# Linear attention and a rational feed-forward layer: the first four attention chunks worked whole, and the decoded words' scratch in PSUM

## The chip, the cores and the metric

The kernel runs on one core of one Trainium2 chip. The metric is the device time of one execution in microseconds, the median of several runs. The core has TensorE (PE; its weight loads are listed as PEld), VectorE (DVE), ScalarE (ACT), GpSimd (POOL) and SyncE (SP, which here issues all data transfers). Each works through its own list of instructions in order and waits on semaphores for the others.

## What is computed

Attention with a decaying state over 4 batches, 8 heads, 768 tokens and 64 dimensions per head, and then a feed-forward layer over the 3072 tokens (512 to 2048 to 512) with a rational function in place of an activation:

```python
for t in range(S):                      # gamma: one decay per head
    state = gamma * state + outer(k[t], v[t])
    y[t] = scale * q[t] @ state
...
h = x @ w_in
P = a[0] + a[1]*h + a[2]*h*h + a[3]*h*h*h
Q = 1.0 + abs(b[0])*abs(h) + abs(b[1])*h*h
out = (P / (Q + 1e-06)) @ w_out
```

## The kernel before

**Attention** goes in 24 chunks of 128 tokens (6 for each batch; `NSTEP`). For chunk i the words of the written order are: `q`/`Q` scale the queries (`scale_q`, on POOL or on DVE), `v` scales the values (POOL), `s` decays the state (POOL), `S` the scores on PE, `M` the causal mask on DVE (PSUM to SBUF), `R` and `r` the recall (state times query) on PE, `V` the masked scores times the values on PE, `O` the outer product of keys and values on PE, `C` the carry of the state on DVE, `X` and `Y` the high and low parts of the result, rounded on ACT and subtracted on DVE. A chunk is cut into two halves of 64 tokens, so that four 64 x 64 matmuls fill the quarters of the PE array, with a state at the beginning (`begin`) and one in the middle (`middle`) of the chunk. The results of 4 chunks are one block of 512 tokens (`x_block`); there are 6 blocks.

**The feed-forward layer** goes in 96 slots: one block of 512 tokens with one of the 16 slices of 128 hidden columns. In slot k, `I` is the first product (`gemm_in`, 12 matmuls into a bank `ph0` or `ph1`), `a`, `b`, `c`, `e` are steps of the rational function on ACT, `p` on POOL, `f` (`poly_vector`) and `H` (`ratio_vector`) on DVE, `g` and `K` split the result into a high and a low part (ACT, POOL), and `Z` is the second product (`gemm_out`, 12 matmuls into the banks `po0` to `po3`), three slots later. `H` ends with the line p (L422), the last reader of the slot's `ph` bank.

**The weights** come as 32 tiles of 64-bit floats. For tile j: `t` reads a byte of each word on ACT (L135), `u` reads the upper word on ACT (L143), `d` joins them on DVE in two operations (L153, u from u and t; L156, t from the raw words and u), `h` rounds on ACT (L166), and `l` takes the rest on POOL (L173). Slot k's `I` needs tiles, `Z` others, in the order of the list `tiles`.

**The order** is written out by hand: `BEGIN` lists the words up to slot 12 with 19 tiles decoded, and each engine gets its instructions in that order. `fill` words are matmuls on zeros whose result nobody reads. After `BEGIN`, `run()` takes the other slots by a rule; there each part of attention stands between two products. On SP a prelude issues the loads of chunks 0 to 5 with `FIRST[i]` weight tiles after chunk i's, up to 11 tiles; later loads are the words `load` and `fetch`, and a load waits on SP until its buffer's last reader is done, with all that stands behind it.

**PSUM** has 8 banks: `po0` to `po3`, `ph0`, `ph1`, and a pair (`pair`). Before, chunks 0 to 3 use `po0`/`po1` and `po2`/`po3` in turn as their pair, the outer products of chunks 0 to 4 use `ph0` and `ph1`, and the scratch `u` of the 19 tiles of `BEGIN` lies in SBUF in buffers of the tag `o`. In `run()` the scratch of the other 13 tiles lies in the pair of the latest chunk (`spare`).

## Time and profile before

| | |
|---|---|
| median of 3 runs | 642.82 us (640.2 to 643.7) |
| the profiled execution | 640.74 us, of it 638.5 us span |
| mean granted TensorE clock | 0.992 |
| PE busy | 606.3 us (95%), 5300 matmul rows |
| DVE busy | 458.9 us (72%), 711 |
| ACT busy | 444.4 us (70%), 723 |
| POOL busy | 363.3 us (57%), 304 |
| data moved | 53.05 MB, mean 83 GB/s |

The span runs from the first to the last instruction. Shares of busy time are means over the whole span; the kernel's beginning and the rest of it look different, so they are read by stage. "A <- B: 5.1" in a list of waits is the idle time of an engine just before A that ended when B was done. A float32 matmul of the attention shows as two rows.

### The profile page before, as it was taken

Reading aid. Unit: us, or ns where it says so; the run is one execution under the profiler, and the core shown is the slowest. Engines: PE = TensorE matmul, PEld = TensorE weight load, DVE = VectorE, ACT = ScalarE, POOL = GpSimd, SP = SyncE. Lnnn points to the kernel's source line nnn. Section 1 sums busy time; section 2 is a strip of 40 time slices with the busy share of each in tenths; the row PEclk is TensorE's granted clock in tenths of the full one; section 3 lists DMA queues with packets and bytes.
Section 4 is the critical chain, followed back from the end, with each engine's and each line's share of the span. In section 5 each row is a group of like instructions: output and inputs, shape, how many; then the busy total and the mean of one; then the engine's idle time right before and its main releaser. Section 6 shows DMA issues by size and latency. Waiting matters only on the chain.

```text
span 638.5 us, 13103 instructions
## 1 busy us (share of the span) xinstructions
PE 606.3 (95%) x5300; PEld 487.2 (76%) x5306; DVE 458.9 (72%) x711; ACT 444.4 (70%) x723; POOL 363.3 (57%) x304
## 2 busy tenths in 40 slices
PE   7588788899999999999999999999999999999997
PEld 3476566688887787788888888888888888888885
DVE  3589999788997776767666666666676666666664
ACT  2278897899987655666667667676666666777773
POOL 3369777688887654546546356545555534444442
PEclk9899899999999999999999999999999999999999
DMA  8958390300302324302202212202121000100001
GB/s 285 377 179 325 135 362 2 132 1 0 132 0 69 124 68 133 128 6 67 67 1 59 80 54 67 69 2 67 47 87 59 3 1 0 39 28 1 2 1 66
DMA packets 24716, 53.05 MB, mean 83 GB/s; under 512 B 3280, under 2 KB 3280, under 8 KB 24656
## 3 DMA queue, kind: packets, MB, share of 16 engines
q1 hardware_dynamic: 24656, 52.22, 23.5%
q8 instruction: 41, 0.67, 0.4%
q14 instruction: 19, 0.16, 0.1%
HBM read 43.82 MB, written 8.39 MB: 82 GB/s over the span
## 4 chain that ended last, share of the span: by engine, by line
PE 75%; DVE 6%; ACT 4%; issue 2%; POOLq 0%; DVEq 0%; ACTq 0%
PE ph L387 36%; PE po L443 35%; PE pair L345 1%; PE pair L297 1%; PE pair L312 1%; PE pair L268 1%; DVE p L411 1%; DVE u L153 1%; DVE q L420 1%; DVE p L422 1%; DVE o L462 1%; ACT s L405 1%; DVE ph L421 1%; ACT p L407 1%; DVE p L412 1%
## 5 line engine op out<-in xcount | busy, mean ns | idle before, releaser
L387 PE MATMUL ph<-xh,w 128*128 128x512 f32 (+2 forms) x776 | 210.6, 393 | 13.8 <-DVE p L422 12.8
L406 POOL TENSOR_TENSOR q<-q,s 128x512 f32<-128x512 f32 x84 | 109.3, 1302 | 198.0 <-ACT s L405 194.3
L443 PE MATMUL po<-w,gh 128*128 128x512 f32 x768 | 199.8, 392 | 0.0
L387 PEld LDWEIGHTS ph<-xh,w 128*128 128x128 f32 x776 | 143.3, 189 | 46.5 <-DVE p L422 14.8
L443 PEld LDWEIGHTS po<-w,gh 128*128 128x128 f32 x768 | 142.8, 188 | 30.2
L411 DVE TENSOR_TENSOR p<-ph,p 128x512 f32<-128x512 f32 x96 | 66.2, 689 | 85.0 <-ACT p L407 84.1
L399 ACT ACTIVATE q<-ph 128x512 f32<-128x512 f32 x84 | 50.2, 597 | 101.4 <-PE ph L387 101.4
L428 POOL TENSOR_TENSOR gl<-p,gh 128x512 fp32r<-128x512 f32 x85 | 110.4, 1299 | 4.7 <-issue 3.3
L443 PE MATMUL po<-w,gl 128*128 128x512 f32 x384 | 110.8, 390 | 1.0 <-POOL gl L533 0.7
L387 PE MATMUL ph<-xl,w 128*128 128x512 f32 (+2 forms) x388 | 104.0, 390 | 0.0
L420 DVE SCALAR_TENSOR_TENSOR q<-q,qcon,ph 128x512 f32<-128x512 f32 x96 | 71.5, 745 | 40.3 <-ACT ph L417 39.1
L443 PEld LDWEIGHTS po<-w,gl 128*128 128x128 f32 x384 | 72.0, 188 | 17.3 <-POOL gl L533 1.7
L387 PEld LDWEIGHTS ph<-xl,w 128*128 128x128 f32 x388 | 73.1, 189 | 15.6
L416 ACT ACTIVATE s<-q,qcon 128x512 f32<-128x512 f32 x96 | 69.5, 724 | 20.8 <-POOL q L406 19.4
L412 DVE SCALAR_TENSOR_TENSOR p<-p,par_sb,ph 128x512 f32<-128x512 f32 x96 | 71.8, 748 | 3.4
L421 DVE SCALAR_TENSOR_TENSOR ph<-p,par_sb,ph 128x512 f32<-128x512 f32 x96 | 71.9, 749 | 0.0
L422 DVE SCALAR_TENSOR_TENSOR p<-q,ph 128x512 f32<-128x512 f32 x96 | 65.9, 686 | 3.3
L417 ACT ACTIVATE ph<-s 128x512 f32<-128x512 f32 x96 | 57.8, 602 | 9.9 <-DVE p L412 0.8
L407 ACT ACTIVATE p<-ph,par_sb 128x512 f32<-128x512 f32 x84 | 64.2, 764 | 0.0
L405 ACT ACTIVATE s<-q,babs 128x512 f32<-128x512 f32 x72 | 58.8, 817 | 2.4
L173 POOL TENSOR_TENSOR w<-t,w 128x512 fp32r<-128x512 f32 x32 | 42.8, 1340 | 25.4 <-ACT w L166 17.5
L427 ACT CAST gh<-p 128x512 fp32r<-128x512 f32 x85 | 52.0, 612 | 7.5 <-DVE p L422 7.2
(55 smaller groups left out, 540.2 us busy)
## 6 DMA issues: line engine op xcount, KB each, us to landing
raw<-in_w_in SPq DMA_DIRECT2D x16, 512.0 KB, 8.0
raw<-in_w_out SPq DMA_DIRECT2D x16, 512.0 KB, 8.4
kT<-in_kT SPq DMA_DIRECT2D x24, 256.0 KB, 4.1
qT<-in_qT SPq DMA_DIRECT2D x24, 256.0 KB, 4.2
v<-in_v SPq DMA_DIRECT2D x24, 256.0 KB, 3.1
out<-o SPq DMA_DIRECT2D x24, 256.0 KB, 2.1
k<-in_k SPq DMA_DIRECT2D x20, 256.0 KB, 3.7
half<-o SPq DMA_DIRECT2D x8, 256.0 KB, 2.4
```

The costliest lines, as they stand in the source:

```text
L387: nc.tensor.matmul(ph[:, t0:t1], w1[f][:, part, kt * P : (kt + 1) * P], x[:, kt, t0:t1], start=(i == 0), stop=(i == 3 * NP - 1),)
L405: nc.scalar.activation(s, q, AF.Identity, bias=babs[:, 0:1], scale=babs[:, 1:2])
L406: nc.gpsimd.tensor_mul(q, q, s)
L407: nc.scalar.activation(p, ph, AF.Identity, bias=par_sb[:, 2:3], scale=par_sb[:, 3:4])
L411: nc.vector.tensor_mul(p, ph, p)
L412: nc.vector.scalar_tensor_tensor(p, p, par_sb[:, 1:2], ph, ALU.add, ALU.mult)
L416: nc.scalar.activation(s, q, AF.Abs_reciprocal_sqrt, bias=qcon[:, 0:1])
L420: nc.vector.scalar_tensor_tensor(q, q, qcon[:, 0:1], ph, ALU.add, ALU.mult)
L421: nc.vector.scalar_tensor_tensor(ph, p, par_sb[:, 0:1], ph, ALU.add, ALU.mult)
L422: nc.vector.scalar_tensor_tensor(p, q, 2.0, ph, ALU.subtract, ALU.mult, reverse0=True)
L428: nc.gpsimd.tensor_sub(gl, p, gh.bitcast(F32))
L443: nc.tensor.matmul(o_tiles[n][tt], g_[:, tt * P : (tt + 1) * P], w2[f][:, part], start=(first and m == 0), stop=(last and m == 2),)
```

## The change

- `by_chunk`: chunks 0 to 3 are worked whole, with new functions. A chunk has 8 matmuls each for scores (64 x 128 by 128 columns), recall, values (128 x 64 by 128) and outer product, one recall in place of two, no middle state, and a mask of 128 x 128 for each head (`causal_sb` is 192 columns wide in place of 64). The masked scores lie in buffers of the tags `p` and `s`.
- PSUM: scores of chunks 0 to 3 lie in `po0` and `po1`, their outer products in `ph0`, their results in the one `pair`; the outer product of chunk 4 lies in `po0` and `po1`; `fill` writes `po3`.
- The scratch `u` of each tile has a bank named in the order (`u6@po0`), or a bank of the latest pair (`pair0`, `pair1`, `half0`).
- `zeros` lies in a buffer of the tag `o`.
- `FIRST`: tile 1 is fetched after chunk 1's loads.
- The queries of chunks 1 to 3 are scaled on POOL (`q1` to `q3`), not on DVE (`Q1` to `Q3`).
- `BEGIN` is a new order of the same slots, chunks and tiles, with 30 fill matmuls in place of 46.

```diff
--- before.py
+++ after.py
@@ -69,18 +69,23 @@
 
     def pair(i):
         if i not in pairs:
-            if 0 <= i < SPB:
-                pairs[i] = [early_bank("pair", f"po{r + 2 * (i % 2)}") for r in range(2)]
-            else:
-                both = early_bank("pair", "pair").rearrange("p (b x) -> p b x", b=2)
-                pairs[i] = [both[:, r] for r in range(2)]
+            both = early_bank("pair", "pair").rearrange("p (b x) -> p b x", b=2)
+            pairs[i] = [both[:, r] for r in range(2)]
+            if i >= SPB:
                 spare.append(both.bitcast(U32))
         return pairs[i]
 
     def u_place(i, place):
 
-        if place is None:
-            return in_halves(ff.tile([P, TB], U32, name="u", tag="o", bufs=BUFS["o"]))
+        if isinstance(place, str) and place[:4] == "pair":
+            if not spare:
+                both = early_bank("scratch", "pair", U32)
+                spare.append(both.rearrange("p (b x) -> p b x", b=2))
+            return in_halves(spare[-1][:, int(place[4:])])
+        if isinstance(place, str) and place not in ("whole", "half0"):
+            return in_halves(early_bank("u", place, U32))
+        if place == "half0":
+            return spare[-1][:, :, : TB // 2]
         if place == "whole":
             return spare[-1][:, i % 2].rearrange("p (b x) -> p b x", b=2)
         return spare[-1][:, :, place * (TB // 2) : (place + 1) * (TB // 2)]
@@ -89,7 +94,7 @@
         return x.rearrange("p (b x) -> p b x", b=2)
 
 
-    causal_sb = const.tile([P, HP], F32, name="causal_sb")
+    causal_sb = const.tile([P, HP + P], F32, name="causal_sb")
     qdec_sb = const.tile([P, NP, P], F32, name="qdec_sb")
     vdec_sb = const.tile([P, H], F32, name="vdec_sb")
     sdec_sb = const.tile([P, NP], F32, name="sdec_sb")
@@ -97,7 +102,7 @@
     babs = const.tile([P, 2], F32, name="babs")
     qcon = const.tile([P, 1], F32, name="qcon")
     lcon = const.tile([P, 1], F32, name="lcon")
-    zeros = const.tile([P, TB], BF16, name="zeros")
+    zeros = ff.tile([P, TB], BF16, name="zeros", tag="o", bufs=BUFS["o"])
     wp = ctx.enter_context(tc.tile_pool(name="wp", bufs=1))
     w1, w2 = {}, {}
 
@@ -257,7 +262,7 @@
     def outer(i):
         if i >= NSTEP:
             return
-        banks = [early_bank("pk", f"ph{b}") for b in range(2)] if i <= SPB else pair(i - 1)
+        banks = [early_bank("pk", f"po{b}") for b in range(2)] if i == SPB else pair(i - 1)
         pk = [x[:, : TB // 2].rearrange("p (h d) -> p h d", d=D) for x in banks]
         st = steps[i]
         st["pk"] = pk
@@ -284,6 +289,88 @@
             steps.setdefault(i + 1, {})["from", 0] = state
             nc.vector.tensor_add(state, st["pk"][1], st["from", 1])
 
+    def whole_outer(i):
+        st = steps[i]
+        st["pk"] = early_bank("pk", "ph0")[:, : TB // 2].rearrange("p (h d) -> p h d", d=D)
+        for aj in range(NP):
+            for r in range(2):
+                h = head(aj // 2, r, aj % 2)
+                nc.tensor.matmul(
+                    st["pk"][half(r), aj], st["k"][:, h], st["v"][:, h],
+                    start=True, stop=True, skip_group_check=True,
+                )
+    def whole_carry(i):
+        state = at.tile([P, NP, D], F32, name="begin")
+        steps.setdefault(i + 1, {})["from", 0] = state
+        if i % C == 0:
+            nc.vector.tensor_copy(state, steps[i]["pk"])
+        else:
+            nc.vector.tensor_add(state, steps[i]["pk"], steps[i]["from", 0])
+    def whole_scores(i):
+        st = steps[i]
+        pa = st["pa"] = [
+            early_bank("pa", f"po{r}").rearrange("p (n t) -> p n t", t=P) for r in range(2)
+        ]
+        for n in range(NP):
+            for r in range(2):
+                nc.tensor.matmul(
+                    pa[r][:, n], st["kT"][half(r), n], st["qT"][half(r), n],
+                    start=True, stop=True, skip_group_check=True,
+                )
+    def whole_mask(i):
+        st = steps[i]
+        for r in range(2):
+            st["aT", r] = ff.tile([P, NP, P], F32, name="aT", tag="ps"[r])
+            nc.vector.tensor_mul(
+                st["aT", r], st["pa"][r],
+                causal_sb[:, HP:].unsqueeze(1).broadcast_to([P, NP, P]),
+            )
+    def whole_px(i, r):
+        return pair(i)[r][:, : TB // 2].rearrange("p (a t) -> p a t", t=P)
+    def whole_recall(i):
+        st = steps[i]
+        for a in range(2):
+            for j in range(2):
+                for r in range(2):
+                    nc.tensor.matmul(
+                        whole_px(i, r)[half(j), a],
+                        st["from", 0][half(r), 2 * a + j], st["qT"][half(r), 2 * a + j],
+                        start=opens(i, r, j), stop=False, skip_group_check=True,
+                    )
+    def whole_values(i):
+        st = steps[i]
+        for a in range(2):
+            for j in range(2):
+                for r in range(2):
+                    nc.tensor.matmul(
+                        whole_px(i, r)[half(j), a],
+                        st["v"][:, head(a, r, j)], st["aT", r][:, 2 * a + j],
+                        start=opens(i, r, j), stop=True, skip_group_check=True,
+                    )
+    def whole_x(i, r):
+        t = slice((i % SPB) * P, (i % SPB + 1) * P)
+        xh, xl = (
+            y.rearrange("p (a r) t -> p a r t", r=2)[:, :, r, t] for y in x_block(i // SPB)
+        )
+        return whole_px(i, r), xh, xl
+    def whole_x_high(i):
+        for r in range(2):
+            x, xh, _ = whole_x(i, r)
+            nc.scalar.copy(xh, x)
+    def whole_x_low(i):
+        for r in range(2):
+            x, xh, xl = whole_x(i, r)
+            nc.vector.tensor_sub(xl, x, xh.bitcast(F32))
     def px(i, kh):
         return pair(i)[kh][:, TB // 2 :].rearrange("p (a r t) -> p a r t", a=2, r=2)
 
@@ -321,7 +408,7 @@
             st["aT", r] = at.tile([P, NP, HP], F32, name="aT")
             x = nc.vector.tensor_mul(
                 st["aT", r], st["pa"][r],
-                causal_sb.unsqueeze(1).broadcast_to([P, NP, HP]),
+                causal_sb[:, :HP].unsqueeze(1).broadcast_to([P, NP, HP]),
             )
             if ordered and r == 1:
                 after(x, st["recalled"])
@@ -493,9 +580,12 @@
 
 
         def fill(n):
-            bank = early_bank("fill", "pair" if SPB not in pairs else "po0")
+            bank = early_bank("fill", "po3")
             for _ in range(n):
-                nc.tensor.matmul(bank[:, :TB], zeros[:, :P], zeros, start=True, stop=True)
+                nc.tensor.matmul(bank, zeros[:, :P], zeros, start=True, stop=True)
+        def by_chunk(whole, halves):
+            return lambda i: (whole if i < SPB else halves)(i)
 
         def gemm_in_begin(k):
             if k == 0:
@@ -548,17 +638,17 @@
             "Q": lambda i: scale_q(i, nc.vector),
             "v": scale_v,
             "s": scale_state,
-            "O": outer,
-            "C": carry,
-            "S": scores,
-            "R": lambda i: recall(i, True),
-            "M": lambda i: mask(i, True),
-            "V": values,
+            "O": by_chunk(whole_outer, outer),
+            "C": by_chunk(whole_carry, carry),
+            "S": by_chunk(whole_scores, scores),
+            "R": by_chunk(whole_recall, lambda i: recall(i, True)),
+            "M": by_chunk(whole_mask, lambda i: mask(i, True)),
+            "V": by_chunk(whole_values, values),
             "r": lambda i: recall(i, False),
-            "X": x_high_both,
-            "Y": x_low_both,
+            "X": by_chunk(whole_x_high, x_high_both),
+            "Y": by_chunk(whole_x_low, x_low_both),
             "t": decode_low,
-            "u": lambda j: decode_high(j, None),
+            "u": decode_high,
             "d": decode_join,
             "h": decode_split,
             "l": decode_rest,
@@ -579,8 +669,9 @@
             "y": lambda k: store_first(k - 1, 1),
         }
         for word in BEGIN.split():
+            word, *place = word.split("@")
             name = word.rstrip("0123456789")
-            emit[name](int(word[len(name) :]))
+            emit[name](int(word[len(name) :]), *place)
 
     def run():
 
@@ -688,25 +779,25 @@
 }
 BUFS = {"gh": 3, "gl": 3, "o": 4}
 FETCH = 11
-FIRST = (1, 0, 1, 1, 2, 2)
+FIRST = (1, 1, 1, 1, 2, 2)
 LAG = 3
 BEGUN = {"slots": 12, "tiles": 19}
 
 BEGIN = """
-t0 u0 d0 h0 Q0 l0 fill18 S0 v0 fill3 O0 n0 v1 C0 s1 fill2 R0 O1 M0 Q1 fill1 V0 v2 r0 S1 C1 X0 Y0
-s2 fill1 R1 O2 M1 Q2 fill2 V1 t1 r1 S2 C2 X1 u1 s3 fill1 R2 Y1 v3 M2 d1 fill3 O3 V2 r2 Q3 h1 C3
-X2 fill1 S3 l1 t2 Y2 R3 s4 u2 M3 v4 d2 fill3 V3 q4 r3 O4 X3 C4 h2 fill1 S4 t3 Y3 l2 I0 u3 t4 s5
-d3 v5 u4 R4 d4 J0 h3 l3 I1 a0 M4 h4 c0 q5 t5 f0 b0 l4 V4 a1 r4 u5 O5 p0 load6 fetch3 c1 C5 X4 d5
-e0 Y4 h5 H0 b1 fill7 S5 l5 R5 t6 p1 t7 M5 u6 fill3 I2 q6 t8 f1 u7 g0 v6 d6 e1 K0 V5 d7 a2 r5 h6
-Z0 load7 fetch1 fetch1 c2 l6 H1 h7 b2 l7 t9 f2 fetch1 O6 g1 p2 I3 X5 C6 u8 K1 e2 Y5 fetch1 d8 v7
-u9 Z1 a3 s7 t10 d9 q7 h8 c3 fetch1 H2 l8 b3 S6 h9 R6 p3 t11 M6 I4 g2 fetch1 l9 f3 u10 u11 K2 t12
-d10 e3 Z2 fetch1 d11 h10 u12 l10 H3 h11 a4 l11 V6 t13 fetch1 r6 b4 O7 load8 d12 I5 c4 p4 X6 C7
-h12 fetch1 f4 s8 g3 l12 u13 t14 Y6 K3 Z3 e4 d13 fetch1 a5 v8 H4 t15 c5 S7 R7 h13 fetch1 b5 M7
-l13 I6 u14 f5 g4 p5 t16 d14 u15 fetch1 K4 e5 Z4 d15 a6 u16 H5 c6 fetch1 b6 V7 r7 h15 p6 O8 f6
-h14 I7 X7 l15 fetch1 g5 d16 e6 l14 Y7 h16 K5 Z5 H6 a7 fetch1 t17 b7 l16 c7 C8 I8 g6 p7 f7 u17
-fetch1 t18 K6 d17 e7 s9 Z6 a8 H7 fetch1 h17 c8 l17 b8 f8 g7 I9 p8 u18 fetch1 d18 K7 e8 h18 Z7 H8
-a9 l18 c9 b9 f9 g8 p9 I10 w8 y8 K8 e9 H9 a10 c10 b10 f10 I11 g9 p10 K9 e10 Z8 a11 H10 c11 b11
-f11 p11 g10 K10 e11 H11 load9 q8 v9
+t0 u0@ph1 d0 h0 Q0 l0 fill20 S0 v0 M0 fill2 O0 v1 V0 C0 s1 O1 X0 C1 q1 Y0 s2 t1 fill4 S1 v2
+u1@po2 R1 M1 n0 O2 d1 V1 q2 X1 C2 fill1 S2 s3 h1 Y1 l1 t2 M2 R2 u2@ph1 v3 d2 fill1 V2 O3 q3 X2
+C3 h2 Y2 s4 t3 fill2 S3 l2 u3@po2 R3 M3 I0 v4 d3 q4 V3 h3 t4 l3 O4 X3 C4 u4@po3 Y3 v5 t5 d4 S4
+u5@po2 s5 J0 d5 q5 h4 R4 I1 a0 c0 M4 l4 h5 f0 t6 l5 b0 V4 u6@po0 r4 p0 O5 t7 load6 fetch3 d6 X4
+u7@po1 C5 Y4 h6 e0 l6 d7 S5 R5 a1 M5 t8 q6 H0 h7 V5 c1 r5 load7 fetch1 fetch1 t9 l7 b1 f1 I2 v6
+u8@po3 g0 d8 p1 u9@po2 fetch1 t10 K0 d9 e1 O6 q7 h8 C6 Z0 h9 fetch1 H1 a2 l8 X5 c2 l9 b2 Y5 I3
+fetch1 g1 f2 s7 u10@pair1 K1 t11 d10 u11@pair0 v7 Z1 t12 fetch1 d11 a3 p2 h10 c3 l10 b3 f3 S6
+fetch1 e2 p3 R6 M6 t13 H2 V6 e3 r6 fetch1 O7 load8 h11 X6 H3 l11 I4 g2 K2 t14 fetch1 C7 g3 Y6 K3
+Z2 a4 u12@pair1 s8 c4 fetch1 d12 v8 b4 u13@pair0 f4 I5 p4 h12 u14@pair1 l12 fetch1 d13 e4 d14
+t15 Z3 h13 a5 H4 l13 fetch1 h14 c5 l14 t16 S7 f5 R7 g4 I6 t17 fetch1 K4 M7 b5 u15@half0 p5 d15
+Z4 a6 fetch1 e5 c6 H5 b6 V7 fetch1 h15 p6 r7 O8 f6 g5 I7 l15 X7 C8 e6 fetch1 K5 Y7 t18 H6 Z5 s9
+a7 u16@pair1 b7 fetch1 d16 c7 p7 g6 I8 u17@pair0 f7 K6 h16 fetch1 u18@pair1 d17 l16 e7 Z6 d18 a8
+h17 c8 l17 H7 b8 h18 p8 f8 g7 I9 l18 e8 K7 H8 Z7 a9 c9 b9 f9 g8 p9 I10 w8 y8 K8 e9 H9 a10 c10
+b10 f10 I11 g9 p10 K9 e10 Z8 a11 H10 c11 b11 f11 p11 g10 K10 e11 H11 load9 q8 v9
 """
 
 
@@ -736,7 +827,9 @@
     par = _np.concatenate([inputs["moe_a"], inputs["moe_b"]])
     gamma = 1.0 - 2.0 ** (-5.0 - _np.arange(H, dtype=_np.float64))
     t = _np.arange(P, dtype=_np.float64)
-    causal = (t[:, None] % (P // 2)) <= t[None, : P // 2]
+    causal = _np.concatenate(
+        [(t[:, None] % (P // 2)) <= t[None, : P // 2], t[:, None] <= t[None, :]], axis=1
+    )
     heads = gamma.reshape(2, 2, 2)
     by_row = _np.repeat(heads.transpose(1, 0, 2).reshape(2, NP), D, axis=0)
     arrays = {
```

## The prediction, made before the changed kernel was run

> **What bounds the kernel now.** I read the busy tenths of the page first, then the busy time by stage, then the chain of waits. One digit below is a fortieth of the span (16 us).
>
> ```profile
> PE   7588788899999999999999999999999999999997
> DVE  3589999788997776767666666666676666666664
> ```
>
> VectorE (DVE) is full in slices 3 to 7, while TensorE (PE) has gaps; from slice 9 PE is full. Cut at the marks that matter (41.04: end of mask M4; 118.24: end of H9, the last rational step ahead of slot 11's product):
>
> ```profile
> core 0: us, PE busy (x) PEld busy (x) DVE busy (x) ACT busy (x) POOL busy (x), PEclk, DMA share, GB/s
> 0.00:12.20 12.20, 8.45 (x98) 3.82 (x99) 3.01 (x8) 3.63 (x6) 3.47 (x7) 1.00 0.86 262
> 12.20:41.04 28.84, 21.37 (x550) 16.75 (x549) 19.16 (x38) 10.43 (x22) 14.70 (x14) 0.88 0.86 317
> 41.04:118.24 77.20, 62.70 (x650) 47.55 (x650) 73.34 (x102) 66.62 (x114) 56.41 (x44) 0.98 0.54 199
> 118.24:183.00 64.76, 64.71 (x285) 53.59 (x286) 55.74 (x82) 57.72 (x95) 52.30 (x46) 1.00 0.14 49
> ```
>
> In the third stage DVE is 95% busy, ScalarE (ACT) 86%, PE 81%. From 118.24 on PE is 100% busy. The chain of waits shows how the one turns into the other (start, us, what):
>
> ```profile
> 94.91 1.66 DVE u L153
> ...
> 117.55 0.70 DVE p L422
> ...
> 118.29 3.02 PE ph L387 x12
> 121.31 2.72 PE po L443 x12
> ```
>
> The chain runs on DVE until p L422, the end of H9, which frees the PSUM bank that slot 11's product waits for; after it, the chain is PE, product after product. So the end is the end of H9 plus PE work that this change leaves alone. What H9 gains or loses, the kernel gains or loses.
>
> **The change part by part.**
>
> *The scratch u of all 19 early tiles moves from SBUF into PSUM banks.* The old kernel holds both forms already, the PSUM one in its later slots (min/median/max in ns):
>
> ```profile
> L153 DVE SCALAR_TENSOR_TENSOR u<-u,t x19: 681/894/1800, 6.1 to 108.3; 128x512 uint32<-128x512 uint32 x19
> L153 DVE SCALAR_TENSOR_TENSOR pair<-pair,t x13: 692/700/700, 130.2 to 197.7; 128x512 uint32<-128x512 uint32 x13
> L156 DVE SCALAR_TENSOR_TENSOR t<-raw,u x19: 691/989/1669, 6.8 to 109.0; 128x512 uint32<-128x512 uint32 x19
> L156 DVE SCALAR_TENSOR_TENSOR t<-raw,pair x13: 686/687/689, 130.9 to 198.4; 128x512 uint32<-128x512 uint32 x13
> L143 ACT ACTIVATE u<-raw x19: 650/670/691, 5.4 to 107.6; 128x512 f32<-128x512 f32 x19
> L143 ACT ACTIVATE pair<-raw x13: 602/614/643, 126.7 to 197.1; 128x512 f32<-128x512 f32 x13
> ```
>
> With u in SBUF the two joins stretch up to 1.8 us; in PSUM they never do. They stretch while GpSimd (POOL) works, whose operation (1.28 undisturbed) stretches too:
>
> ```profile
> 34.31 1.28 POOL L173 TENSOR_TENSOR w<-t,w 128x512 fp32r<-128x512 f32 x1 [3.93 <-ACT w L166]
> 38.09 1.73 POOL L173 TENSOR_TENSOR w<-t,w 128x512 fp32r<-128x512 f32 x1
> 38.72 1.66 DVE L156 SCALAR_TENSOR_TENSOR t<-raw,u 128x512 uint32<-128x512 uint32 x1
> ```
>
> POOL is 81% busy (52.30 of 64.76) in the stage that holds most of the PSUM joins, so they are steady beside a busy neighbour. Sums over the first 185 us (x19) and over the third stage (x14), busy us and mean ns:
>
> ```profile
> L156 DVE SCALAR_TENSOR_TENSOR t<-raw,u 128x512 uint32<-128x512 uint32 x19 | 21.1, 1110 | 0.9
> L153 DVE SCALAR_TENSOR_TENSOR u<-u,t 128x512 uint32<-128x512 uint32 x19 | 20.2, 1063 | 5.0 <-ACT u L143 5.0
> L156 DVE SCALAR_TENSOR_TENSOR t<-raw,u 128x512 uint32<-128x512 uint32 x14 | 16.4, 1170 | 0.7
> L153 DVE SCALAR_TENSOR_TENSOR u<-u,t 128x512 uint32<-128x512 uint32 x14 | 15.5, 1108 | 0.1
> ```
>
> A PSUM pair of joins costs 0.700 + 0.687 = 1.387 us. All 19: 41.3 - 26.4 = 14.9 us off DVE; 31.9 - 14 x 1.387 = 12.5 of it in the third stage, 2.5 before. ACT saves 0.056 us a tile.
>
> *Chunks 0 to 3 whole.* Each mask is 2 operations of 512 columns in place of 256, the carry one operation in place of two, and the q scaling of chunks 1 to 3 goes from DVE to POOL.
>
> ```profile
> L322 DVE TENSOR_TENSOR aT<-pair,causal_sb 128x256 f32<-128x256 f32 x16 | 6.0, 416 | 3.0 <-PE pair L297 3.0
> L227 DVE TENSOR_TENSOR qT<-qT,qdec_sb 128x512 f32<-128x512 f32 x4 | 2.7, 684 | 0.0
> L281 DVE TENSOR_TENSOR middle<-pk,begin 128x256 f32<-128x256 f32 x4 | 1.7, 424 | 6.3 <-PE pair L297 5.1 <-PE pk L268 1.3
> L227 POOL TENSOR_TENSOR qT<-qT,qdec_sb 128x512 f32<-128x512 f32 x5 | 7.4, 1473 | 0.0
> ```
>
> The 512-column mask is not in the trace: it lies between 0.416 (no longer than now) and 2 x 0.416 = 0.83; I take 0.684, the other 512-column multiply. DVE: masks 8 x 0.268 = +2.1, carries 4 x -0.424 = -1.7, scaling 3 x -0.684 = -2.1. POOL gets at most 3 x 1.47 = 4.4 more in a stage where it had 14.70 of 28.84, so there it becomes as tight as DVE. On PE scores, values, outer and the two recalls go from 16 matmuls each (recalls 8 + 8) to 8, but scores and values now also compute the 64-token cross blocks, twice the product. PE isn't the bound there, so I take zero and keep both ends below. All four chunks now share one pair of banks (they alternated over po0 to po3): recall i+1 waits for the low half (Y) of chunk i, with values and outer behind it on PE; the longer mask on DVE covers that (0.7 us if not).
>
> *What the opening waited for.* The idle time of DVE between 12.20 and 41.04 is 28.84 - 19.16 = 9.7 us (us in total, times, longest):
>
> ```profile
> DVE middle L281 <- PE pair L297: 5.1, 2, 4.4
> DVE aT L322 <- PE pair L297: 3.0, 1, 3.0
> DVE middle L281 <- PE pk L268: 1.3, 1, 1.3
> PE pair L297 <- issue: 3.2, 1, 3.2
> q8 instruction: 41, 0.67, 0.4%
> PE 606.3 (95%) x5300; PEld 487.2 (76%) x5306; DVE 458.9 (72%) x711; ACT 444.4 (70%) x723; POOL 363.3 (57%) x304
> ```
>
> These are waits for PE, and PE itself once stood 3.2 us in the middle of one recall, waiting for nothing shown. The instruction queue q8 moved 41 packets for 10,606 PE and weight-load rows, 259 each: I read the stall as a packet of PE instructions that was late behind the data transfers (DMA share 0.86). A whole chunk has half the rows (some 128 in place of 256), so two of four packets go. [...]
>
> So M4's end: 41.0, less DVE work (2.5 stretch, 2.1 scaling, 1.7 carries, minus 2.1 masks, minus 1.4 for the joins of tile 5, which now stand ahead of M4) = 2.8, less about half of the 9.4 us of waits, as the rows halve: 33.5. Bounds: 38 (waits stay) and 29. The floor is the loads: ahead of chunk 4's last byte lie 4 raw tiles (one more than before, tile 1's fetch is moved ahead of chunk 2 on SP's queue and delays chunks 2 to 4 by 0.5 MB), 5 chunks of 1.05 MB, the decay table and the mask, now 0.1 MB: 7.7 MB; 3.2 MB land by 12.2 at 262 GB/s and the rest at 317 to 400 by 24 to 26, then q4, scores and mask add 3. Chunk 5's loads wait for chunk 1's values, which don't come later.
>
> *The third stage.* DVE: 73.34 - 12.5 - 1.4 (tile 5) = 59.4. ACT: one tile's three operations and one linear term stand ahead of M4 now (2.4 start to start), and 13 x 0.056 = 0.7: 66.62 - 3.1 = 63.5. POOL: below 56.41. PE: 62.70, less two fills. ACT is the longest now: what goes off DVE is not all won, since ACT is next at 63.5. Two engines that feed each other, both near full, will not do as well as one: I take ACT at 95%, what DVE reached: 66.8. Bounds: 64.5 and 63.5 / 0.86 = 73.6 (ACT no better used than now).
>
> *The rest.* BEGIN issues the same loads, fetches, slots and tiles, in another order; load6, load7 and load8 still stand behind V4, V5, V6 and the fetches behind them, and move with these. Fills fall by 16 matmuls; they only filled gaps (if the clock sinks for that: a 3.9 us gap is in the old trace too). The zeros tile and the fill bank po3 cost nothing: po3 is next used by tile 4's u, after the last fill. outer of chunk 4 uses po0 and po1, whose masks are done. After H9 the order is unchanged: zero, 0 to 2 us if ACT is behind there.
>
> *Sum.* H9 ends at 33.5 + 66.8 = 100.3 in place of 118.24: 17.9 us less. The profiled execution took 640.74 (span 638.5 and 2.2 around it), 2.1 below the median of 642.82. 640.7 - 17.9 = 622.8.
>
> **The rivals.**
>
> *ACT becomes the bound as loosely as it is used now.* For: it must serve DVE, PE and POOL in one fixed order; it waited on DVE 86% used. Against: much of its idle time was waiting for stretched joins. Stage 73.6: H9 at 107.1, 629.6.
>
> *The opening stays as late as its waits.* Either PE stalls for its instructions as before, or it pays for the new shapes. After an attention block a product takes 2.95 in place of 2.72 us:
>
> ```profile
> 301.80 2.95 PE ph L387 x12
> 304.75 2.72 PE po L443 x12
> ```
>
> A whole chunk changes shape about four times (64 x 128, 64 x 64, 128 x 64, fills): 16 x 0.23 = 3.7 us. M4 then ends at 37.5 to 38, H9 at 105: 627.3. [...]
>
> *The scratch banks serialize ACT and DVE, and it is slower.* From tile 10 on u alternates over pair0 and pair1, and its write on ACT must wait until the joins of the tile before it in that bank are done; behind it in ACT's queue stand a, b, c, e of the slots. If each of 13 tiles cost ACT a full turn, 1.39 + 0.61 = 2.0 us, the stage is 63.5 + 26 = 89.5, H9 at 123: 645.5. It turns to a loss once a tile costs over 1.7 us. Against: where the old kernel has u in the pair, DVE waited little for it:
>
> ```profile
> DVE pair L153 <- ACT pair L143: 6.1, 12, 1.2
> ```
>
> 0.5 us each, and tiles 6 to 9 have four banks.
>
> *No change:* only if the joins stretch in PSUM too in this stage; then 12.5 us come back and the opening's gain is half lost: 639.
>
> **How the numbers follow.** Forecast 623: 0.62, own range 616 to 628. ACT loose, 630: 0.17. Late opening, 627: 0.11. Serialized, 645: 0.06. No change: 0.04. Half a per cent (3.2 us) is about what a measurement of this kernel can tell from none. Faster 0.90, same 0.04, slower 0.06. The range takes in the first three with their bounds: low 616 (M4 at 30, stage 64.5: 23.7 less is 617, and one for the run), high 634 (M4 at 38 with a stage of 73.6: 634.1).
>
> **What would show it.** Joins at 0.69 to 0.70 us with little spread right from the start; POOL's operations at 1.3. M4 ending at 30 to 36; no long PE stall inside chunks 2 and 3. Between M4 and H9 ACT at least as busy as DVE, 65 to 70 us long. I11 starting near 100, and PE solid from there. The prediction is wrong if the joins stretch against POOL with PSUM operands; if ACT stands before its u writes waiting for DVE's joins; or if PE shows idle time after I11 that it did not have.

## The result and the profile after

The changed kernel takes 632.44 us (631.41 to 634.66, 4 runs) beside 641.51 us for the kernel before in the same comparison: ratio 0.986, 95% interval 0.982 to 0.991. It is 1.4% faster, clear of the noise and inside the outer range of 616 to 634, but outside the 616 to 628 that went with the forecast of 623: 9 us were won where 18 were forecast. The profiled execution took 634.66 us (span 632.9), 2.2 above the median.

Page of the changed kernel, busy tenths of PE, DVE and the granted clock:

```profile
PE   8779898999999999999999999999999999999997
DVE  3668788789887766766667667666666666766663
PEclk9978899999999999999999999999999999999999
```

Busy time by stage, cut at the same marks (M4 now ends at 37.78, H9 at 112.15; columns as before: PE, PEld, DVE, ACT, POOL, granted clock, DMA share, GB/s):

```profile
0.00:12.20 12.20, 10.50 (x86) 5.50 (x86) 4.08 (x9) 3.68 (x7) 4.15 (x8) 1.00 0.79 263
12.20:37.78 25.58, 19.66 (x293) 15.83 (x291) 15.97 (x32) 12.26 (x26) 17.75 (x17) 0.91 0.97 357
37.78:112.15 74.37, 64.26 (x647) 50.96 (x646) 60.26 (x101) 63.91 (x110) 49.27 (x41) 0.92 0.57 207
112.15:183.00 70.85, 70.79 (x312) 58.55 (x313) 61.02 (x91) 63.37 (x105) 57.84 (x51) 1.00 0.14 45
```

From H9 to the end lie 632.9 - 112.15 = 520.8 us, before 638.5 - 118.24 = 520.3: the end is H9 plus a constant, as the prediction had it. DVE has 60.26 us of work in the third stage (59.4 forecast), ACT 63.91 (63.5). The work was forecast right. The stage is 74.4 long in place of 66.8, M4 4.3 late, H9 11.9 late.

The joins and POOL's operation (min/median/max in ns):

```profile
L158 DVE SCALAR_TENSOR_TENSOR pair<-pair,t x22: 692/700/700, 59.9 to 191.6; 128x512 uint32<-128x512 uint32 x22
L158 DVE SCALAR_TENSOR_TENSOR u<-u,t x10: 690/692/700, 5.7 to 51.7; 128x512 uint32<-128x512 uint32 x10
L161 DVE SCALAR_TENSOR_TENSOR t<-raw,u x10: 686/688/701, 6.4 to 52.5; 128x512 uint32<-128x512 uint32 x10
L178 POOL TENSOR_TENSOR w<-t,w x32: 1272/1292/1328, 7.9 to 197.1; 128x512 fp32r<-128x512 f32 x32
```

The stretch is gone, on both engines, from the first tile on. What got worse is the clock: 0.92 in the third stage in place of 0.98. Four PE operations of the timeline (idle time and its releaser in brackets), the granted clock behind them (PE busy, clock, DMA share, GB/s), and two products of the chain of waits:

```profile
32.81 0.76 PE L399 MATMUL pair<-qT,kT 64*64 64x64 f32 x32 [1.98 <-POOL begin L250]
45.26 0.69 PE L399 MATMUL pair<-qT,kT 64*64 64x64 f32 x32 [2.53 <-DMA k<-in_k]
47.10 1.13 PE L432 MATMUL pair<-aT,v 64*64 64x64 f32 x32 [0.92 <-DVE aT L409]
66.55 0.69 PE L432 MATMUL pair<-aT,v 64*64 64x64 f32 x32 [1.99 <-DVE aT L409]
```

```profile
34.00:38.00 4.00, 4.00 (x30) 0.50 0.62 247
50.00:54.00 4.00, 4.00 (x11) 0.53 1.01 364
66.00:70.00 4.00, 3.13 (x75) 0.68 0.43 131
```

```profile
49.15 5.16 PE ph L474 x12
...
112.21 3.02 PE ph L474 x12
```

PE stands 2.0 to 2.5 us before S4, S5 and V6, where the new order has no fills (the old one had one ahead of S4, seven ahead of S5 and none ahead of V6). Behind S4 the clock is granted at half until 40 us (0.50 from 34 to 40), and behind V6 for the next 3 to 4 us (0.50 from 68 to 70, 1.00 from 71 on); behind S5 it stays near full (0.96 from 45.3 to 47.1) until a second gap, 0.92 us before V5, and is half from there to 54 us (0.50 from 47.1 to 50, then 0.53). Product I2 takes 5.16 us in place of 3.02. The releaser named for S5 is doubtful: in this trace and in those of experiments 4 and 6 S5 starts 0.26 us after Y4 ends on DVE, the last reader of the pair that S5 writes.

### The profile page after: what moved, and what is told of

It is laid out like the page before. It is cut to its first block, busy times and chain, and to the rows that moved or that the text cites. A ratio compares the mean times of both kernels' runs of the same rounds, so it can differ in the third digit from the quotient of the medians.

```text
span 632.9 us, 12567 instructions
## 1 busy us (share of the span) xinstructions
PE 608.2 (96%) x5032; PEld 491.4 (78%) x5034; DVE 443.5 (70%) x704; ACT 443.9 (70%) x723; POOL 360.2 (57%) x307
## 4 chain that ended last, share of the span: by engine, by line
PE 78%; DVE 8%; ACT 4%; issue 2%; POOLq 0%; POOL 0%; DVEq 0%; ACTq 0%
PE ph L474 38%; PE po L530 35%; PE pair L432 1%; PE pair L384 1%; PE pair L273 1%; PE pair L399 1%; DVE q L507 1%; DVE ph L508 1%; DVE pair L158 1%; DVE p L509 1%; DVE p L498 1%; DVE t L161 1%; DVE o L549 1%; ACT s L492 1%; ACT pair L148 1%
## 5 line engine op out<-in xcount | busy, mean ns | idle before, releaser
L474 PE MATMUL ph<-xh,w 128*128 128x512 f32 (+2 forms) x776 | 213.6, 398 | 6.4 <-DVE p L509 5.3
L474 PEld LDWEIGHTS ph<-xh,w 128*128 128x128 f32 x776 | 145.9, 192 | 39.3 <-DVE p L509 7.8
L530 PEld LDWEIGHTS po<-w,gh 128*128 128x128 f32 x768 | 142.8, 188 | 30.2
L474 PE MATMUL ph<-xl,w 128*128 128x512 f32 (+2 forms) x388 | 105.4, 394 | 0.0
L507 DVE SCALAR_TENSOR_TENSOR q<-q,qcon,ph 128x512 f32<-128x512 f32 x96 | 71.5, 745 | 41.8 <-ACT ph L504 40.6
L474 PEld LDWEIGHTS ph<-xl,w 128*128 128x128 f32 x388 | 74.4, 193 | 15.9
L503 ACT ACTIVATE s<-q,qcon 128x512 f32<-128x512 f32 x96 | 69.3, 722 | 21.7 <-POOL q L493 19.2
L499 DVE SCALAR_TENSOR_TENSOR p<-p,par_sb,ph 128x512 f32<-128x512 f32 x96 | 71.8, 748 | 3.4
L178 POOL TENSOR_TENSOR w<-t,w 128x512 fp32r<-128x512 f32 x32 | 41.3, 1295 | 20.0 <-ACT w L171 12.1
```

The lines of the kernel that those rows point to most:

```text
L474: nc.tensor.matmul(ph[:, t0:t1], w1[f][:, part, kt * P : (kt + 1) * P], x[:, kt, t0:t1], start=(i == 0), stop=(i == 3 * NP - 1),)
L499: nc.vector.scalar_tensor_tensor(p, p, par_sb[:, 1:2], ph, ALU.add, ALU.mult)
L503: nc.scalar.activation(s, q, AF.Abs_reciprocal_sqrt, bias=qcon[:, 0:1])
L507: nc.vector.scalar_tensor_tensor(q, q, qcon[:, 0:1], ph, ALU.add, ALU.mult)
L530: nc.tensor.matmul(o_tiles[n][tt], g_[:, tt * P : (tt + 1) * P], w2[f][:, part], start=(first and m == 0), stop=(last and m == 2),)
```

## The experiments

Times are medians, ratios go against the kernel before of the same comparison. "Stage" is M4 to H9 in the profiled execution. DVE lines have other numbers in some kernels.

**1. The scratch alone, in the old order and halves.**

```diff
-u3 ... u4 ... u8 ... u9 ... u18
+u3@po1 ... u4@po2 ... u8@half0 ... u9@pair0 ... u18@pair1   (13 of 19 tiles)
```

> The old order, halves and loads as before; the scratch u of 13 of the 19 early tiles lies in PSUM (tiles 3 to 10, 13, 14, 15, 17, 18), which are the ones whose joins stretched most: in the old trace their 26 joins took 11.4 us more than 0.69 to 0.70 us each. Theory A (the stretch of the joins against POOL was what VectorE lost, and it was the bound): VectorE's busy time between M4 and H9 falls by about 11 us and H9 comes 7 to 11 us earlier, limited by ScalarE at 66 us in that stage; time about 632 to 635, that is nearly all that the whole change brought. Theory B (the new order and the whole chunks bring the gain, the joins only overlap better): within 2 us of the old kernel, 640 to 643.

636.17 us, ratio 0.993 [0.991, 0.995]. DVE has 63.97 us in the stage (73.34 before), H9 ends at 113.6, 4.6 earlier, where theory A asked for 7 to 11. Nine microseconds less work on DVE gave half of that.

**2. The new order, scratch back in SBUF.**

```diff
+ if place is None: return in_halves(ff.tile([P, TB], U32, name="u", tag="o", ...))
- u3@po2 ... u18@pair1
+ u3 ... u18
```

> The new kernel with its order, its whole chunks and its loads, but with the scratch u of all 19 early tiles back in SBUF (four buffers). Theory A: the joins stretch again to 0.9 to 1.1 us in the mean, 10 to 15 us more VectorE work ahead of H9, and the gain goes: 638 to 646. Theory B: joins stretch, but ScalarE and TensorE bound the stage, so the time stays at 632 to 635.

639.52 us, ratio 0.998 [0.996, 1.000]: without the scratch in PSUM nearly nothing is left. DVE is back at 70.51 in the stage, but the clock is 0.87 there, so the price of the scratch is mixed with the clock's (experiment 12 parts them). Here and in experiment 12 `zeros` is a tile of its own again, 128 columns wide, which a fill reads four times over.

**3. The new order and scratch, chunks 0 to 3 in halves.**

```diff
- "S": by_chunk(whole_scores, scores), "M": by_chunk(whole_mask, ...), ...
+ "S": scores, "M": lambda i: mask(i, True), "V": halves_values, ...
```

> The new order, loads and PSUM scratch, but chunks 0 to 3 worked in halves of 64 tokens as before (outer products in po0 and po1, scores in the pair; C0 and R0 stand ahead of M0). Theory A1 (whole chunks save packets of TensorE instructions, 3 us): M4 ends some 3 us later, 635 to 636. Theory A2 (whole chunks cost TensorE more array time than they save): each chunk's products take about 0.7 us less on TensorE, time within 2 us of the new kernel's 632, or below it.

640.59 us (636.4 to 643.7), ratio 0.998 [0.995, 1.001], slower than both theories have it. M4 ends at 40.0, at a clock of 0.85 up to there. Again the clock is mixed in.

**4. The changed kernel with 26 more fills at the new gaps.**

```diff
-d4 S4 ... d7 S5 ... h7 V5 ... f1 I2
+d4 fill8@ph0 S4 ... d7 fill10@po3 S5 ... h7 fill4@po3 V5 ... f1 fill4@po3 I2
```

> The new kernel with 26 more matmuls on zeros, where TensorE stood idle in the new trace: 8 ahead of S4 (bank ph0), 10 ahead of S5, 4 ahead of V5, 4 ahead of I2 (bank po3). Theory C (the new order lost 5 to 6 us to the halved TensorE clock: I1 took 4.4, I2 5.2, in place of 2.9): granted clock between 30 and 62 us near 1.0, I1 and I2 at 2.9 to 3.1, time 626 to 629. Theory D (these products only fill time in which VectorE and ScalarE are late anyway): clock up, but H9 within 1.5 us of the new kernel's 112, time 631 to 634.

629.89 us (629.07 to 630.47), ratio 0.983 [0.981, 0.985]. The granted clock of its profiled execution, at the places where it had been half:

```profile
34.00:38.00 4.00, 4.00 (x76) 1.00 0.69 270
50.00:54.00 4.00, 4.00 (x17) 1.00 1.03 409
62.00:66.00 4.00, 3.67 (x48) 0.57 0.58 190
```

M4 ends at 34.57, I2 takes 3.02. Only behind V6, where this kernel has no fills, the clock still falls. H9 ends at 106.9, 5.2 us earlier; the time lies between theory C's 626 to 629 and theory D's 631 to 634, nearer to C.

**5. The changed kernel once more.**

> The changed kernel as it is, once more, so that the next three stand beside it on one chip. All theories: 631 to 635, with H9 near 112 in the profile. If the halved clock of TensorE between 33 and 54 us is chance (it varies from execution to execution), the runs spread wider than those of the kernel with more fills (1.4 us there), by 3 us or more.

632.15 us, ratio 0.986 [0.983, 0.990], single runs from 629.1 (mean clock 0.992) to 637.6 (0.981). With fills they spread over 1.4 us. The profiled execution took 630.77 us, and M4 ends at 34.28 in it. It has the gap before S4 again:

```profile
30.88 0.69 PE L399 MATMUL pair<-qT,kT 64*64 64x64 f32 x32 [1.98 <-POOL v L238]
```

Here the clock is 1.00 up to 34.28 us, and the next product of 512 columns begins with four matmuls in 1.20 us; above, the same kernel had 0.50 from 34 to 38 us, and the same four took 2.07. So the same gap lost the clock in one execution and not in the other, and the fills are worth about 2.3 us of median.

**6. Fills, and q6, q7, v6, v7 later on POOL.**

```diff
-t8 q6 H0 ... I2 v6
-u8@po3 g0 d8 p1 u9@po2 ... K0 d9 e1 O6 q7 h8 ... v7 Z1 ... p2 h10
+t8 H0 ... I2
+u8@po3 g0 d8 p1 v6 u9@po2 ... K0 q6 d9 e1 O6 h8 ... Z1 ... p2 q7 v7 h10
```

> The kernel with 26 more fills, and on GpSimd the scaling of chunk 6's and 7's queries (q6, q7) and of v6 and v7 behind the squares p1 and p2 in place of ahead of them. Theory L (GpSimd stood 2.8 and 1.2 us before q6 and q7 for loads that SP could issue only after V4 and V5, and p1, p2, the rests and low parts queued behind): p1 starts 1.5 to 2.5 us earlier, H9 2 to 4 us earlier than 106.9, time 626 to 628. Rival (the slots wait for ScalarE anyway): H9 within 1 us, time 629 to 631.

627.77 us, ratio 0.979 [0.977, 0.981]. In experiment 4 the list of waits from 30 to 60 us held

```profile
POOL qT L232 <- DMA raw<-in_w_in: 2.8, 1, 2.8
...
ACT s L503 <- POOL q L610: 1.5, 1, 1.5
```

q6 stood on POOL for a load that was late, with l7, v6 and the square p1 behind it, and ACT's e1 behind that. The old order has p1 ahead of q6, and p2 ahead of v7 and q7; the new one had turned them round. Both rows are gone here. H9 moves from 106.9 to 105.0.

**7. Fills, u11, u13, u17 ahead of the joins whose pair they share.**

```diff
-d10 u11@pair0 ... d12 v8 b4 u13@pair0 ... d16 c7 p7 g6 I8 u17@pair0
+u11@pair0 d10 ... u13@pair0 d12 v8 b4 ... u17@pair0 d16 c7 p7 g6 I8
```

> The kernel with 26 more fills, and the scratch reads u11, u13 and u17 (bank 0 of the pair) ahead of the joins d10, d12 and d16 (bank 1 of the same pair) in the order. Theory P (the two banks of a pair count as one tile, so these three reads on ScalarE waited for a join in the other bank, and the slots behind them): ScalarE no longer waits for the join ahead of these three, H9 1 to 3 us earlier than 106.9, 627 to 629. Rival (they had slack): within 0.7 us, 629 to 631.

630.06 us, ratio 0.983 [0.981, 0.985], H9 at 107.0: no effect. That ACT waits for the joins of the other bank of the pair (1.38 us before u11 in the changed kernel) is not what holds the stage.

**8. Fills, and chunks 0 to 3 in halves.** The edits of experiments 3 and 4 together.

> The kernel with 26 more fills, and chunks 0 to 3 in halves of 64 tokens. The halves without more fills gave 640.6 with runs from 636 to 644, at a clock of 0.98, so clock and halves were mixed there. If the whole chunks bring time by themselves: 3 us or more above the whole chunks with fills (629.9), 633 to 637, and M4 some 3 us later than 34.6 at full clock. If the halves only lost to the clock: 629 to 631.

636.07 us, ratio 0.990 [0.988, 0.993]. The first row is its opening, the second that of experiment 4:

```profile
0.00:39.53 39.53, 30.21 (x642) 20.32 (x643) 19.52 (x44) 15.53 (x31) 21.83 (x25) 0.87 0.87 313
```

```profile
0.00:34.57 34.57, 29.45 (x383) 20.40 (x387) 19.96 (x40) 15.67 (x31) 21.51 (x25) 1.00 0.94 333
```

Working the chunks whole is worth 6 us of median and 5 of the opening, with 383 rows on PE in place of 642 and busy times on every engine that differ by less than 0.8 us. The halves' opening has a lower clock too (0.87), and C0 and R0 had to go ahead of M0, so not all 5 us need be the halves' own.

**9. Which engine sets the third stage: one engine's work cut at a time.** On the kernel of experiment 6.

```diff
act: -nc.scalar.activation(s, q, ...)             slots 2 to 11, POOL squares q*q
dve: -scalar_tensor_tensor(u, u, 3, t, ...)       tiles 8 to 17
pe:  -((0, xh), (0, xl), (1, xh)) +((0, xh), (0, xl))   products I4 to I10
```

> The order with fills and later q6, q7 (e6), and one ACT operation fewer per slot: the affine b is left out for slots 2 to 11 (the square on POOL multiplies q by q instead), 8 x 0.70 = 5.6 us of ACT between M4 and H9. Nothing else changes. Theory A (the third stage is as long as ACT's work at 90%): the stage falls from 70.8 to 64.6 and H9 from 105.0 to about 99, 622. Theory P (PE sets it): H9 104 to 105, 627 to 628. Theory L (no engine sets it but the path of a slot, product, a, b, p, e, H, which frees the bank for the product after the next): each slot's path is 0.7 shorter, half of that a slot with two banks, H9 about 102, 625.

> The same kernel as e6, and 7.0 us of DVE less: the first join (0.70 us) is left out for tiles 8 to 17, all between M4 and H9. Theory A: ACT stays as it is, H9 within 1 us of 105.0, 627 to 628. Theory P: the same. Theory L: DVE's queue is emptier, so f and H start earlier behind the joins, 0.3 to 0.7 a slot, H9 at 100 to 103, 623 to 626. If DVE itself sets the stage, 7 us less: H9 at 98, 621.

> The same kernel as e6, and 7.0 us of PE less ahead of H9: the products I4 to I10 leave out the term of xl (8 of 12 matmuls, 28 x 0.25 us). Theory A: H9 within 1 us of 105.0, 627 to 628, and PE has 7 us more gaps. Theory P: H9 at 98 to 99, 621. Theory L: each product is 1.0 shorter on the path, half of it a slot: H9 101 to 102, 624.

Measured: ACT less 629.56 us (0.979 [0.977, 0.982]), DVE less 626.12 (0.975 [0.972, 0.977]), PE less 629.62 (0.980 [0.978, 0.982]). The cuts leave out the step b of each slot, the first of a tile's two joins, and one of the three terms of the first product. The PE cut leaves out the term xh with the weights' low part, not xl as its expectation says; the time is the same 28 matmuls. Stage lengths: 71.8, 68.1 and 70.3. With ACT cut, I4 took 5.49 us, four matmuls 1.91 to 2.07 in place of 1.07 to 1.20; the same kernel uncut, in an execution with the same 5.49 and a clock of 0.57 to 0.58 from 60 to 68 us (experiment 11), has 72.4. So 5.7 us less on ACT gave 0.6. 6.5 us less on DVE gave 2.1 to 2.7, beside 70.2 (experiment 10) and 70.8 (experiment 6) with all work. 7 us less on PE gave 0.5 beside experiment 6, and 2.1 beside the 72.4, since its I4 was slow too (2.08 us for the first four matmuls, clock 0.88 from 62.9 to 75.8 us). In the times only DVE's cut shows. Theory A, that the stage is ACT's work at some fixed share, falls, and so does theory P, that PE sets it.

**10. M6 ahead of f3**, on the kernel of experiment 6.

```diff
-b3 f3 S6 fetch1 e2 p3 R6 M6 t13
+b3 S6 fetch1 R6 M6 f3 e2 p3 t13
```

> The same kernel as e6, all work kept, and on DVE the mask M6 stands ahead of f3 (and R6 ahead of e2 and p3 in the order written). PE stood 2.0 us before V6 for this mask, and the clock fell to 0.70 in the 5 us after. Theory G (that gap and its slow product are on the path): V6 starts 1.5 us earlier, I4 3.0 in place of 3.5, H9 at 103, 626. Theory A (ACT sets the stage): no change, 627 to 628.

629.84 us, ratio 0.981 [0.979, 0.984]; stage 70.2. PE waits 0.85 us before V6 now, and I4 takes 3.04, but I4 waits 2.03 us for H2, which stands behind f3:

```profile
60.38 0.69 PE L432 MATMUL pair<-aT,v 64*64 64x64 f32 x32 [0.85 <-DVE aT L409]
63.80 1.20 PE L474 MATMUL ph<-xh,w 128*128 128x512 f32 x4 [2.03 <-DVE p L509]
```

The gap has moved by one step, and the time stays.

**11. Two and three engines cut together**, and their base once more.

> Both cuts in one kernel: the affine b of slots 2 to 11 (5.6 us of ACT) and the first join of tiles 8 to 17 (7.0 us of DVE) are left out. Alone each left the stretch from H4 to H9 within 0.6 us of its 30.2. Theory B (ACT, DVE and PE are so evenly loaded in this order that another is next wherever one is cut): together the stage falls to about what PE needs, 64.3 at 95%, 67 to 68, and H4 to H9 to 28. Theory L (the path of a slot and its two banks set the pace): b and a join are off each path, about 0.7 a slot, H4 to H9 about 27. Theory N (something else, which neither cut touches, a wait in POOL's queue or a bank of the scratch): H4 to H9 stays within 1 us of 30.2, the stage within 1.5 of the cut on DVE alone, 68.1.

> The three cuts together: ACT 5.6 us less, DVE 7.0, and PE 7.0 (the term of xl left out of I4 to I10). Theory B: all three engines are 10% shorter, and so is the stage: 70.8 x 0.9 = 64, H4 to H9 26 to 27. Theory L: 1.7 us off each slot's path, half of it a slot, H4 to H9 about 25 to 26. Theory N: H4 to H9 still 29 to 30.

> The kernel of e6 once more, as the base of this set. If M4's end differs from execution to execution by the speed of the loads alone (34.2 in e6, 35.5 to 36.1 in the four after it, whose opening is the same code, with a DMA share of 0.97 and 0.95 to 0.97), it lies between 34 and 36.5 here, and M4 to H9 within 0.7 of 70.8. Median 627 to 630.

624.39 us (0.972 [0.970, 0.973]), 623.55 (0.971 [0.970, 0.972]), and the base 628.74 (0.979 [0.977, 0.980]). The base's stage is 72.4 long, not within 0.7 of 70.8 as expected: its I4 took 5.49 us, in experiment 6 3.55. The stage cut at H4, for the kernel before, the changed one, experiment 6, and the one with all three cuts:

```profile
41.04:86.50 45.46, 35.37 (x462) 26.42 (x462) 42.92 (x59) 39.36 (x68) 35.12 (x28) 0.96 0.67 240
86.50:118.24 31.74, 27.33 (x188) 21.13 (x188) 30.42 (x44) 27.26 (x46) 21.29 (x17) 1.00 0.37 141
```

```profile
37.78:82.00 44.22, 37.55 (x459) 29.66 (x459) 34.41 (x60) 37.55 (x66) 30.79 (x26) 0.86 0.78 285
82.00:112.15 30.15, 26.71 (x188) 21.30 (x188) 25.85 (x42) 26.36 (x45) 18.49 (x16) 1.00 0.25 93
```

```profile
34.22:74.80 40.58, 37.53 (x476) 28.21 (x474) 34.38 (x59) 37.43 (x66) 30.71 (x26) 0.96 0.86 326
74.80:105.00 30.20, 26.73 (x188) 21.29 (x188) 25.87 (x42) 26.36 (x45) 18.49 (x16) 1.00 0.24 90
```

```profile
34.61:71.90 37.29, 34.91 (x420) 25.80 (x418) 29.73 (x52) 34.28 (x62) 28.41 (x25) 0.95 0.88 323
71.90:100.64 28.74, 23.70 (x217) 18.18 (x216) 23.79 (x39) 24.00 (x41) 19.75 (x18) 1.00 0.35 134
```

Up to H4 the three engines are 85 to 92% busy together. The cut on DVE alone brings this stretch from 40.6 (40.0 in experiment 10) to 37.9, with ACT's to 37.1, and all three to 37.3: nearly all of it is DVE's. From H4 to H9 the length is 31.7 before, 30.5 in experiment 1 (old order, scratch in PSUM), 30.2 to 30.3 in every kernel that kept the new order there with its work and PSUM scratch, 29.6 to 30.2 with one cut, 29.4 with ACT's and DVE's, and 28.7 with all three. There 8 to 11% less work on PE, DVE and ACT together took 5% off, and left them 82 to 84% busy. Theory N's 29 to 30 comes nearest and is missed by 0.3; theories B and L asked for 25 to 27. So no single engine's load sets this stretch. The chain of waits shows what does from H4 to H5; first experiment 6, then the kernel with all cuts (whose line numbers are higher):

```profile
74.83 3.05 PE ph L474 x12
77.88 0.02 issue
77.90 0.60 ACT q L602
78.50 0.62 ACT s L503
79.12 0.02 issue
79.14 0.61 ACT ph L504
```

```profile
73.18 0.52 ACT gh L625
...
73.83 1.30 POOL gl L628
75.13 1.01 POOL q L615
...
76.16 0.74 ACT s L507
```

In the first, ACT's a6 waits for product I6, which waits for H4, and e5 (s L503) stands behind a6 in ACT's queue although it needs nothing of slot 6; H5 waits for e5. That place alone costs only some 0.3 us, because e5 also needs p5, which ends on POOL at 78.18. p5 stands behind K4 on POOL and needs b5, which stands behind g4 on ACT, and K4 and g4 both need H4. With the product shortened, this way by K4 and p5 is the chain itself. So H5 waits for H4 by two ways through the order of a queue, within 0.3 us of each other. The later slots of the stretch were not taken apart like this.

**12. The scratch in SBUF at full clock** (the edit of experiment 2 on the kernel of experiment 6).

> The kernel of e6 (fills, later q6 and q7), with the scratch u back in SBUF: the price of the scratch alone at full clock. By the sums of the joins 15 us more on DVE, 12 of them after M4. Theory B (three engines evenly loaded): DVE is then the longest, 72 us of work at 92 to 95% as in the kernel before, stage 76 to 78 in place of 70.8, 634 to 636. If every microsecond of DVE counts: stage 82, 640. If the place of the scratch hardly matters at full clock: 628 to 631.

639.10 us, ratio 0.996 [0.994, 0.998], beside the base's 628.74 in the same comparison: 10.4 us. First its stage and its joins from 34 to 119 us (busy us, mean ns), then the base's stage:

```profile
37.64:118.78 81.14, 65.59 (x655) 50.26 (x654) 71.68 (x101) 63.96 (x110) 54.38 (x41) 0.94 0.52 189
```

```profile
L160 DVE SCALAR_TENSOR_TENSOR u<-u,t 128x512 uint32<-128x512 uint32 x14 | 17.5, 1248 | 2.7 <-ACT u L150 2.7
L163 DVE SCALAR_TENSOR_TENSOR t<-raw,u 128x512 uint32<-128x512 uint32 x14 | 16.0, 1144 | 0.8
```

```profile
34.06:106.49 72.43, 65.80 (x664) 50.37 (x662) 60.24 (x101) 63.78 (x111) 49.38 (x42) 0.95 0.60 224
```

11.4 us more work on DVE make the stage 8.7 longer, and M4 3.6 later. That is nearest to the expectation that every microsecond of DVE counts: with the scratch in SBUF, where DVE is 88% busy, most of its extra work lengthens the stage, while with the scratch in PSUM 6.5 us less on it won 2.1 to 2.7. The fills and the later q6 and q7, worth 3.4 to 4.7 us with the scratch in PSUM, are worth about 1 us here (experiment 2: ratio 0.998; this one: 0.996).

**13. Other orders of the queues between H4 and H9**, all work kept.

```diff
 first:  -h13 a5 H4 ... g4 ... b5 u15@half0 p5 d15 Z4 a6 e5 c6 H5
         +h13 a5 b5 H4 l13 p5 ... g4 ... e5 u15@half0 H5 d15 Z4 a6 c6
         (and b7 p7 e7 H7 ahead of u17 h16 d17, b9 p9 e9 H9 ahead of I10 w8 y8)
 second: +h13 a5 b5 H4 ... l14 p5 ... K4 M7 u15@half0 d15 Z4 e5 a6 c6 H5
         (and b9 ahead of c9, w8 y8 behind H9)
```

> The kernel of e6 and e15 with all its work, and another order in the queues of slots 5, 7 and 9 between H4 and H9. There the changed order has, on ACT, a6 (which waits for product I6, and so for H4) ahead of e5; h16 and u18 (which wait for joins) ahead of e7; and the two copies of w8 ahead of e9. On POOL K4 stands ahead of p5, and on DVE the joins d17 and d18 ahead of H7. Here b5, p5, e5, H5 and b7, p7, e7, H7 and b9, p9, e9, H9 go ahead of these. Theory Q (the order of the queues sets the pace of these slots, not the load of an engine): H4 to H9 falls from 30.2 towards PE's own 26.7, to 27 to 28.5, H9 about 103, 625 to 627. Theory B (evenly loaded engines): it stays within 0.7 of 30.2, 628 to 629, or grows where another queue now waits.

> A smaller swap of the same kind on the kernel of e6 and e15, after e17 shortened H4 to H5 (5.7 in place of 7.2), H6 to H7 (6.4 in place of 8.0) and H8 to H9 (4.3 in place of 5.8) and lost it again between (H5 to H6 7.1 in place of 4.9, H7 to H8 8.4 in place of 4.3), where d15, and K7 behind two low parts, came too late. Here only b5, p5 and e5 go ahead of a6 (d15 stays ahead of H5), b9 ahead of c9, and w8 and y8 behind H9. Theory Q: H4 to H5 about 6, H8 to H9 about 5, the pieces between them as in e6, H4 to H9 28 to 29, 626 to 628. If each microsecond won comes back at the next piece as in e17: 30.2, 628 to 629.

The first: 633.84 us, ratio 0.987 [0.984, 0.989], 5 us slower than the base. H4 to H9 takes 31.9 us, and its span ends 632.1 - 107.2 = 524.9 after H9 in place of 520.6, since a product waits for H10, which ends at 116.9 (110.5 in experiment 6, whose H9 ends 2.2 earlier): slot 10 came late because Z7 on PE waited 1.3 us for ACT's g7 and 2.1 for POOL's K7. Behind these gaps two matmuls of Z7 take 1.05 us in place of 0.62, and the clock is 0.91 from 74 to 112 us where the base has 1.00 from 76 to 106.5, so part of the 5 us is the clock's. The second: 628.53, ratio 0.980 [0.978, 0.983], H4 to H9 29.4: 0.8 us won in the profile, no difference in the times. Both lengths lie outside what theory Q asked for (27 to 28.5, and 28 to 29). From H4 to H5 alone they take 5.8 and 6.5 us in place of 7.2, as it asked, but later slots lose what was won. The order of the queues moves this stretch and what follows by 5 us with the same work, by waits and by the clock behind them; an order that makes it much shorter was not found. Of the kernels that keep all work, experiment 6 is the best, 2.1% under the kernel before in both of its comparisons.

## Why the prediction was right in direction and wrong in size

*The scratch: right.* Joins cost what the PSUM rows of before said, and DVE's 59.4 came out as 60.3. The scratch is worth 5.3 us of median in the old order (13 of the 19 tiles) and 10.4 in the new one with the fills. Experiments 1, 2 and 12 agree: 0.69 to 0.70 us with PSUM (1), means of 0.97 to 1.25 in the third stage without (2 and 12). Why DVE and POOL slow each other with the scratch in SBUF, no run shows.

*Whole chunks: right in place.* The opening is 5 us shorter than with halves, the clock's share included (0.87 with halves, 1.00 whole), and a mask of 512 columns takes 0.69 us, as assumed. That the packets of instructions were the reason is not shown. q8 moved 39 in place of 41, as forecast, and the stall of 3.2 us is gone; but with halves experiments 3 and 8 have no such stall either: their longest PE gaps from 20 to 50 us are 1.98 and 1.41 us, and each ends with a releaser, DVE's xl and POOL's begin.

*M4 at 33.5: right, with a spread.* M4 ends at 34.1 to 34.9 in seven of the executions with fills and at 35.5 to 37.0 in five others with the same opening, four of them at full clock. Without fills it ends at 37.8 in one profiled execution, at half clock behind S4 (0.50), and at 34.3 in the other, where the clock held (1.00).

*"The rest" failed first.* "Fills fall by 16 matmuls; they only filled gaps" was costed at nothing, with the clock named in brackets and waved off by one gap of the old trace. That gap is no comfort: behind its 3.88 us, at 69.00 us, four matmuls took 2.08 us in place of 1.19, and the clock was 0.70 from 70 to 74. Fills were the cover: without them 2.3 to 2.5 us of median, and 7 us in the profiled execution together with the loads. A gap of 1.98 us before S4 was enough for a clock of 0.50 in one execution of the changed kernel, and in another the same gap left it at 1.00 (experiment 5): how long a gap may be is not shown.

*The same part, "load6, load7 and load8 still stand behind V4, V5, V6 and the fetches behind them, and move with these".* The loads moved less than the work did: M4 came 3.3 us earlier and load6 0.9. And the new order put q6 ahead of p1 on POOL, which the prediction did not look at. So q6 stood for its load and held p1, and with it e1: about 2.1 us (experiments 4 and 6).

*"The third stage" failed last and for most.* "I take ACT at 95%." ACT reached 90% with clock and loads mended, and cutting its work gave 0.6 us, so ACT was not the bound. The stage is two stretches: to H4, where DVE, ACT and PE are 85 to 92% full together and only DVE's cut won time, and from H4 to H9, which no single engine's load sets. Spread over both in the proportion of before, the forecast of 66.8 asked for 39.3 and 27.5. Experiment 6 has 40.6 and 30.2. Between H4 and H9 DVE lost 4.6 us of work and the stretch 1.5. That the order of the queues sets this stretch is shown from H4 to H5, by the chain and by experiment 13 (7.2 us to 5.8 and 6.5). For the later slots it is argued.

*The sum of the gap:* forecast 622.8, measured 632.4. Clock 2.5 (experiment 4), loads 2.1 (6), and of the 5 left (627.8) 2.7 from H4 to H9, 1.2 ahead of H4, 0.7 at M4. The kernel of experiment 6 took 1 us more when it was run again, so each of these is known to about 1 us. Of the rivals, "ACT loose" came nearest in time, and its stage of 73.6 was near the 74.4 measured; that was luck, because its reason is refuted. "Late opening" had M4's 37.5 to 38 right for the profiled execution, by the clock rather than by changed shapes, since the same kernel has 34.3 at full clock (experiment 5); the scratch banks did not serialize (ACT waited 1.4 us for joins, once). That rival's turning point works out to 1.6 us a tile from its own terms, not 1.7.

What stays open: an order for slots 5 to 9 that gives the 30.2 us back, what holds the stretch ahead of H4, and why M4 differs by up to 3 us between executions at the same code.
